# Top-k attention with a routed MLP on one core: where a batch's first block is transposed, and when reciprocals of row sums are taken

## Chip, core and metric

One core of a Trainium2 chip runs the whole kernel. The metric is device time in microseconds (us), the median of several runs. TensorE is PE in the profile (PEld its weight loads), VectorE is DVE, ScalarE is ACT, GpSimd is POOL and SyncE is SP. A "q" behind a name (SPq) is the engine's queue of DMA issues and waits.

## What is computed

Two stages in float32. First attention over 8 batches, 8 heads, 576 rows, head size 64, where each row keeps only its 32 largest scores. Then each of the 4608 rows (512 wide) goes to one of 8 experts, a two-layer MLP of width 1024, and is scaled by the gate's weight.

```python
def _attn_ref(q, k, v):
    scores = scale * np.matmul(q, k.transpose(0, 1, 3, 2))
    kth = np.partition(scores, -top_k, axis=-1)[..., -top_k:-top_k + 1]
    scores = np.where(scores >= kth, scores, -1000000000.0)
    attn = np.exp(scores - np.max(scores, axis=-1, keepdims=True))
    attn = attn / (np.sum(attn, axis=-1, keepdims=True) + 1e-09)
    return np.matmul(attn, v)

def _moe_ref(x, w_gate, w1, w2):
    logits = x @ w_gate
    expert_idx = np.argmax(logits, axis=1)
    ...
    for e in range(E):
        h = np.maximum(x_sorted[lo:hi] @ w1[e], 0.0)
        y_sorted[lo:hi] = h @ w2[e]
    ...
    return gate_w[:, None] * y
```

## The kernel before, in words

**The two stages are interleaved.** The attention's work is cut into 144 slots, 18 for each batch: a slot is two tiles of 128 query rows, as a rule the same rows of the two heads of a "unit" (4 units a batch; one slot in nine takes the remaining 64 rows of both heads of two units). As soon as a batch's rows are finished they are sorted by expert into a table in DRAM (x_rows), and full blocks of 128 rows of one expert are run through the MLP in between the slots of the next batches. What is left over when the attention is done runs behind it.

**A slot** i of the main loop `loop()` (lines 916 to 972) goes through these steps, and each engine gets its instructions in that order:
- DVE: `fold` (L290, L292: maximum h and minimum l of two halves of the scores s), then `search`: 8 MAX8 (L338) with MATCH_REPLACE8 (L345) between them find the 32nd largest score of each row; `fold_on` (L298, L300) prepares the next slot before the last round. Between these, `tick()` puts in one small instruction of other work at a time, from the list `aside`.
- ACT: `low` (L354) from DVE's threshold, two relu passes (L370); POOL: two subtractions (L379) that mark what is not kept.
- ACT: copies of the scores of slot i + 3 from PSUM (L283).
- PE: `turning(i - 1)`, the transposition of the previous slot's weights (wTm L398, with ACT's copies wT L404 or L402; then wTl, L411 or L409, with the copy wTt L419 or L417).
- PE: a few `pieces` of the current MLP block, in two helpings before and one behind the next steps.
- ACT: `weights`, the exponentials (L387) with row sums z.
- PE: `multiply(i + 4)`, scores of a later slot (sc L276).
- In some slots a step of `ending` (from line 803) of a finished unit: products with v (po L432, copy oT L434), the transposition back and the gate's logits (px L443, copy xl L450), `divisors` (ACT rz L454 and L455, DVE reciprocal L457), and on POOL `logits` and `rows` (L465 to L478) that multiply by the reciprocals.

PE, ACT and DVE run in the order in which the loop writes their instructions; SP's order of DMA issues follows from the same order. There are three slots of scores in advance (AHEAD = 3), so DVE may run ahead of PE and ACT until it needs an s (L290) that ACT has not copied; and ACT may run ahead of DVE until it needs a threshold (L354).

**An MLP block** (`block`, L673) has 16 pieces. Its rows xg must first be transposed by PE (`turned`: xtp L662) and copied to SBUF by ACT (xTs L664). Then come 8 pieces of the first layer (ph L687, copy hT L692), and 8 of the second (py L702, scaled copy y L716, scattered to the output by POOL, L708). Copies that ACT owes to a block wait in a list `due` and are written down by `evacuate()`. In the middle of a block `following()` transposes the rows of the next one, if its load is old enough (`landed`, 3 slots). For the first block of a batch there is no block before it that could do so; then `block` itself calls `turned`, yields "pause", and its next step starts with `evacuate("xT")`. This happens in slot 13 of a batch, in the helpings ahead of `weights`.

**Loads** on SP: for each block xg (L642) and two weight tiles w (L634, L636), issued by `ahead()` when the block before the last one loaded begins; for each unit qkb (L141) and vb (L245).

**Divisors.** In `ending`, `next(div)` writes ACT's two rz instructions, and `aside.append(div)` at once puts the DVE reciprocal on the list, so that it goes into the next search. `through(div)` at the place "rows" makes sure that it has been written before POOL's `logits`.

Of the kernel before, what the change touches and what calls it, by code (L numbers as in the profile page):

```python
# [35 lines left out]
def kernel(  # L36
# [265 lines left out]
    aside = []  # L302
# [365 lines left out]
    def evacuate(upto=None):  # L668

        while due and (upto is None or upto in [kind for kind, _ in due]):  # L670
            due.pop(0)[1]()
# [62 lines left out]
    with fast:  # L734
# [10 lines left out]
        current = None  # L745
        left = clock = 0

        def landed(n):
            return clock is None or clock - n.at >= ON_CHIP
# [16 lines left out]

        def following():
            put_stores()
            if loaded and landed(loaded[0]):
                turned(loaded[0])  # L770

        def pieces(n):
            nonlocal current, left
            while n > 0 and left > 0:
                if current is None:
                    if not landed(loaded[0]):
                        break
                    current = block(loaded.pop(0), following, stores.append)
                    ahead()
                if clock is None:  # L780
                    evacuate()
                step = next(current)
                if step == "pause":
                    if clock is not None:
                        break
                    continue
                if step == "last":
                    current = None
                n -= 1
                left -= 1  # L790
            return n
# [11 lines left out]
        def ending(b, u):  # L803

            nonlocal left
            n = unit[b * U + u]
            if u == 0:
                x_of[b] = k.xp.tile([P, KC, XW], F32, name="x")
                in_turn(token_ids(x_of[b][:, :, Dm + 1].bitcast(I32), b))
                lg_of[b] = k.small.tile([P, KC, E], F32, name="lg")  # L810
            x, lg = x_of[b], lg_of[b]
            out_steps = outputs(n, x)
            yield "products"
            next(out_steps)
            yield "relu"
            next(out_steps)
            if u % 2 == 0:
                yield "relu"
            div = divisors(n)
            next(div)  # L820
            aside.append(div)
            yield "products"
            next(out_steps)
            if b * U + u + 2 < len(units):
                load_values(unit[b * U + u + 2])
            yield "relu"
            next(out_steps)
            yield "products"
            next(out_steps)
            yield "relu"  # L830
            next(out_steps, None)
            yield "rows"
            through(div)
            logits(n, lg)
            rows(n, x)
            if u < U - 1:
                return
            yield "small"
            r = choice(lg)
            aside.append(r.steps)  # L840
            yield "weights"
            yield "turn"
            through(r.steps)
            nc.scalar.activation(lg, lg, AF.Exp)
            yield "products"
            ranks(r)
            yield "small"
            steps = places(r, x)
            aside.append(steps)
            yield "relu"  # L850
            nc.scalar.copy(run, r.run)
            yield "pool"
            through(steps)
            scatters.extend(scattering(r, x))
            if b == B - 1:
                scatter(KC)
                slot_i = k.small.tile([1, 2, NSLOT], I32, name="slot_i")
                through(table(slot_i, SURE, False))
                firsts = [(slot_i[0:1, 0, j:j + 1], slot_i[0:1, 1, j:j + 1]) for j in range(SURE)]
                ready = load_rows(SimpleNamespace(), firsts[0][1], True)  # L860
            new = LAST - SURE if b == B - 1 else new_of[b]
            if new:
                slot_i = slot_last if b == B - 1 else k.small.tile([1, 2, NSLOT], I32, name="slot_i")
                steps = table(slot_i, new, b == B - 1)
                aside.append(steps)
                yield "weights"
                yield "pool"
                yield "weights"
                yield "pool"
                through(steps)  # L870
                coming.extend((slot_i[0:1, 0, j:j + 1], slot_i[0:1, 1, j:j + 1]) for j in range(new))
            if b == B - 1:
                spare.extend(coming[ALWAYS - SURE:])
                del coming[ALWAYS - SURE:]
                assert len(loaded) == 2 and not waiting
                fill_up()
                coming[0:0] = [(firsts[0][0], ready)] + [(expert, (piece,)) for expert, piece in firsts[1:]]
                scatter(0)
# [27 lines left out]
        def loop():  # L906
            nonlocal credit, rate, clock
            for i in range(min(AHEAD, len(work))):
                multiply(i)
                s_of[i], steps = scores(got_of.pop(i))  # L910
                for step in steps:
                    step()
            multiply(AHEAD)
            f_of[0] = fold(s_of[0])
            fold_on(f_of[0])
            for i, (b, g) in enumerate(work):
                tiles = tiles_of(i)
                u, tile = g[0]
                if tile == 0 and u % 2 == 0:
                    open_unit(tiles[0][0])  # L920
                if tails(tiles):
                    open_unit(tiles[1][0])

                then = lambda: None
                if i + 1 < len(work):
                    f_of[i + 1] = fold(s_of[i + 1])
                    then = lambda: fold_on(f_of[i + 1])
                low, nbias, doubts = search(tiles, s_of[i], f_of.pop(i), then)
                at_place("small")
                w_of[i] = depths(s_of[i], low)  # L930
                less(s_of.pop(i), w_of[i])
                doubts()
                put_stores()
                scatter(1)
                at_place("pool")
                at_place("relu")
                at_place("rows")
                at = i % per_batch
                if at == FIRST and b:
                    rate = new_of[b - 1] * PIECES / (U * NT)  # L940
                credit += rate * len(g)
                room = left
                if b == B - 1 and at >= ARRIVED:
                    room -= KEEP
                    credit = room / (len(work) - i)
                share = {0: 0.5, 1: 1.2, 2: 1.6, 3: 0.5, 2 * NC: 1.4}[tile]
                now = max(0, min(int(credit * share + 0.5), room))
                credit -= now
                clock = i
                if i + AHEAD < len(work):  # L950
                    s_of[i + AHEAD], steps = scores(got_of.pop(i + AHEAD))
                    for step in steps:
                        step()
                evacuate()
                at_place("turn")
                turns = turning(i - 1) if i else iter(())
                next(turns, None)
                part = min(BETWEEN, now - now // 2)
                rest = pieces(part)
                next(turns, None)  # L960
                rest = pieces(now - now // 2 - part + rest)
                weights(tiles, w_of[i], nbias)
                next(turns, None)
                evacuate()
                if i + AHEAD + 1 < len(work):
                    multiply(i + AHEAD + 1)
                if tile == NC - 1:
                    end = ending(b, u)
                    late.append([end, next(end)])
                at_place("products")  # L970
                at_place("weights")
                credit = min(credit + pieces(now // 2 + rest), 6 * rate)

            for _ in turning(len(work) - 1):
                pass
            assert len(late) == 1
            clock = None
            for place in late[0][0]:
                if place == "rows":
                    pieces(4)  # L980
            kept = left - ALWAYS * PIECES
            assert kept >= 0, kept
            k.apart = True
            pieces(kept)
# [135 lines left out]
```

## Time and profile before

| what | value |
|---|---|
| runs before, us | 1373.47, 1373.48, 1373.33, 1374.39 (median 1373.48) |
| the profiled execution | 1374.84 us, span of its instructions 1373.2 us |
| busy PE / DVE / ACT / POOL | 1232.6 / 1084.2 / 931.8 / 661.3 us |
| granted PE clock, mean | 0.953 |
| the last search ends | 1090.8 us; what follows is MLP blocks |
| HBM traffic | 208.72 MB read, 22.33 MB written |

Busy shares in 40 slices are tenths (9 is 90% or more), each slice 34.3 us. A line of the timeline has the start, the duration, engine, line, operation, output<-input, shapes and count, and in brackets the idle time of the engine before it and what ended it. PE's counts are twice those of the program, since each float32 matmul is two instructions in the trace. The chain of waits that ended last covers only the last 28 us (it begins at 1344.85) and lies within the last MLP blocks.

### The profile page before, as it was taken

To read this page: it belongs to the slowest core of one execution; us is meant where nothing else is said; L and a number is where in the kernel's file an instruction comes from. 1 tells how busy PE (TensorE), PEld (TensorE's weight loads), DVE (VectorE), ACT (ScalarE), POOL (GpSimd) and SP (SyncE) were. 2 spreads that over 40 slices of the span, in tenths; PEclk is the share of its full clock that TensorE was granted. 3 is DMA by queue.
4 is the path that set the end of the run, shared out by engine and by line. 5 is a ranking of instruction groups with operands and counts; after the bars stand their busy time and mean duration, and the time that the engine had idled before them with its cause. 6 is when DMAs were issued, how large, how long until landed. Compare 5 with 4: busy or idle time off the path is not lost. (4 is left out here: it accounts for less than half of the span.)

```text
span 1373.2 us, 24487 instructions
## 1 busy us (share of the span) xinstructions
PE 1232.6 (90%) x7666; PEld 839.0 (61%) x7666; DVE 1084.2 (79%) x4591; ACT 931.8 (68%) x2113; POOL 661.3 (48%) x805
## 2 busy tenths in 40 slices
PE   5777677677799999999999999999999999999995
PEld 3444444444467666767676666667676676776773
DVE  7999999999999999999999999999999720000000
ACT  4788877877888888887877788887777821111110
POOL 3455547555654666566556655665556621000000
PEclk9788887888999999999999999999999999999998
DMA  2000011001573277427554573367443759999880
GB/s 82 29 29 29 28 36 55 29 29 44 185 290 135 76 252 253 151 64 265 214 193 148 183 276 131 110 214 283 166 167 110 272 182 357 388 323 329 304 319 19
DMA packets 102221, 231.68 MB, mean 169 GB/s; under 512 B 5183, under 2 KB 25919, under 8 KB 102081
## 3 DMA queue, kind: packets, MB, share of 16 engines
q1 hardware_dynamic: 95328, 209.76, 43.6%
q0 software_dynamic: 6464, 19.97, 4.0%
q8 instruction: 62, 1.02, 0.3%
q14 instruction: 79, 0.64, 0.1%
q10 hardware_dynamic: 288, 0.30, 0.1%
HBM read 208.72 MB, written 22.33 MB: 168 GB/s over the span
## 5 line engine op out<-in xcount | busy, mean ns | idle before, releaser
L379 POOL TENSOR_TENSOR w<-s,w 128x576 f32<-128x576 f32 x288 | 409.6, 1443 | 432.0 <-ACT w L370 432.0
L687 PE MATMUL ph<-xTs,w 128*128 128x128 f32 x2560 | 308.6, 276 | 7.2 <-ACT xTs L664 6.0
L687 PEld LDWEIGHTS ph<-xTs,w 128*128 128x128 f32 x2560 | 297.4, 192 | 27.7 <-issue 18.4
L702 PE MATMUL py<-w,hT 128*128 128x512 f32 x640 | 292.2, 596 | 0.0
L338 DVE MAX8 tops<-scr 128x8 f32<-128x168 f32 x864 | 245.8, 316 | 0.0
L276 PE MATMUL sc<-qkb 64*128 64x288 f32 (+1 forms) x1280 | 220.1, 469 | 9.7 <-ACT s L283 5.2
L387 ACT ACTIVATE w<-w,nbias 128x576 f32<-128x576 f32 x288 | 223.9, 791 | 3.5 <-POOL w L379 2.5
L370 ACT ACTIVATE w<-s,low 128x576 f32<-128x576 f32 x288 | 207.6, 768 | 4.7
L398 PE MATMUL wTm<-turn,w 128*128 128x128 f32 x1152 | 173.2, 291 | 34.7 <-ACT xl L450 21.6
L398 PEld LDWEIGHTS wTm<-turn,w 128*128 128x128 f32 x1152 | 135.1, 148 | 95.2 <-issue 35.5
L999 DVE CAST any_i<-pd 1x1 int32<-1x1 f32 x1 | 0.1, 147 | 237.4 <-PE pd L997 237.4
L702 PEld LDWEIGHTS py<-w,hT 128*128 128x128 f32 x640 | 114.4, 190 | 117.6 <-issue 116.5
L345 DVE MATCH_REPLACE8 scr<-tops,scr 128x168 f32<-128x168 f32 x576 | 177.2, 312 | 0.0
L283 ACT COPY s<-sc 128x576 f32<-128x576 f32 x288 | 169.0, 640 | 10.6 <-PE sc L276 10.6
L404 ACT COPY wT<-wTm 128x512 f32<-128x512 f32 x256 | 139.3, 603 | 39.4 <-PE wTm L398 39.0
L276 PEld LDWEIGHTS sc<-qkb 64*128 64x128 f32 (+1 forms) x1280 | 117.9, 195 | 72.8 <-issue 25.5
L432 PE MATMUL po<-wT,vb 128*64 128x288 f32 x1024 | 157.1, 455 | 0.4 <-ACT wTt L419 0.4
L708 POOL DMA_INDIRECT out_dram<-y,xg x40 | 43.1, 1078 | 212.9 <-ACT y L716 199.6
L329 DVE MAX8 few<-l 128x8 f32<-128x288 f32 x288 | 127.4, 442 | 0.0
L692 ACT ACTIVATE hT<-ph 128x512 f32<-128x512 f32 x80 | 48.6, 608 | 108.7 <-PE ph L687 108.7
L290 DVE TENSOR_TENSOR h<-s 128x576 f32<-128x576 f32 x144 | 117.1, 813 | 5.9 <-ACT s L283 5.9
L432 PEld LDWEIGHTS po<-wT,vb 128*64 128x64 f32 x1024 | 74.9, 151 | 76.2 <-issue 28.1
(116 smaller groups left out, 1430.7 us busy)
## 6 DMA issues: line engine op xcount, KB each, us to landing
w<-in_moe_w_dram SPq DMA_DIRECT2D x80, 2048.0 KB, 9.6
qkb<-in_qk_dram SPq DMA_DIRECT2D x31, 608.0 KB, 4.4
xg<-x_rows SPq DMA_DIRECT2D x40, 257.0 KB, 10.0
vb<-in_v_dram SPq DMA_DIRECT2D x32, 320.0 KB, 3.2
x_rows<-blank SPq DMA_DIRECT2D x5, 257.0 KB, 15.8
x_rows<-blank POOLq DMA_DIRECT2D x4, 257.0 KB, 9.1
x_rows<-x,posi POOLq DMA_INDIRECT x40, 3.2
out_dram<-y,xg POOLq DMA_INDIRECT x40, 6.1
```

Of the source, the lines that this page charges most:

```text
L276: nc.tensor.matmul(ps[rows, j, 0:HF], n.q[d, cols], n.k[d, keys], start=True, stop=True)
L283: lambda m=m, ps=ps: nc.scalar.copy(s[:, m, :, :], ps[:, :, 0:HF]) for m, ps in enumerate(got)
L338: nc.vector.max(out=tops[:, m, r * 8:(r + 1) * 8], in_=src[m])
L345: nc.vector.match_replace(out=scr[:, m, :], in_to_replace=tops[:, m, r * 8:(r + 1) * 8], in_values=src[m], imm_value=NEG,)
L370: nc.scalar.activation(w[:, m, :], s[:, m, :, :].rearrange("p j k -> p (j k)"), AF.Relu, scale=-STEEP, bias=low[:, m:m + 1],)
L379: k.last_pool = in_turn(nc.gpsimd.tensor_tensor(w[:, m, :], s[:, m, :, :].rearrange("p j k -> p (j k)"), w[:, m, :], op=ALU.subtract)).ins
L387: nc.scalar.activation(w[:, m, :], w[:, m, :], AF.Exp, scale=scale, bias=nbias[:, m:m + 1], accum_out=n.z[:, c:c + 1])
L398: nc.tensor.transpose(pm[:, c * P:(c + 1) * P], w[:, m, first:first + P], ident)
L404: nc.scalar.copy(wT[:, :, m, q], pm4)
L432: nc.tensor.matmul(po[r, 0:HF], n.v[:, c, r], rhs, start=(c == 0), stop=(c == KC - 1))
L687: nc.tensor.matmul(ph[:, f, :], n.w1[:, 0, dt, fc * P:(fc + 1) * P], n.xT[:, dt, :], start=(dt == 0), stop=(dt == DT - 1),)
L702: nc.tensor.matmul(py, hT[:, f, :], n.w2[:, 0, f, :], start=(f == 0), stop=(f == FT - 1))
```

## The change

Three places. `following()` no longer transposes rows that are transposed already, and the loop calls it in each slot in which no block is running. `pieces` begins a block inside the loop only if its rows have been transposed (after the loop `block` does it, as before). And the reciprocal of `divisors` is put on the list two steps later in `ending`.

```diff
--- before.py
+++ after.py
@@ -766,14 +766,14 @@
 
         def following():
             put_stores()
-            if loaded and landed(loaded[0]):
+            if loaded and landed(loaded[0]) and not hasattr(loaded[0], "xT"):
                 turned(loaded[0])
 
         def pieces(n):
             nonlocal current, left
             while n > 0 and left > 0:
                 if current is None:
-                    if not landed(loaded[0]):
+                    if clock is not None and not hasattr(loaded[0], "xT"):
                         break
                     current = block(loaded.pop(0), following, stores.append)
                     ahead()
@@ -818,13 +818,13 @@
                 yield "relu"
             div = divisors(n)
             next(div)
-            aside.append(div)
             yield "products"
             next(out_steps)
             if b * U + u + 2 < len(units):
                 load_values(unit[b * U + u + 2])
             yield "relu"
             next(out_steps)
+            aside.append(div)
             yield "products"
             next(out_steps)
             yield "relu"
@@ -961,6 +961,8 @@
                 rest = pieces(now - now // 2 - part + rest)
                 weights(tiles, w_of[i], nbias)
                 next(turns, None)
+                if current is None:
+                    following()
                 evacuate()
                 if i + AHEAD + 1 < len(work):
                     multiply(i + AHEAD + 1)
```

From line 964 on the line numbers are two higher in the changed kernel.

## Prediction

> **What bounds the kernel now.** I read the page's busy slices first. VectorE is full up to the 27th slice and idle behind it; TensorE is full from about the 12th slice to the end.
>
> ```profile
> PE   5777677677799999999999999999999999999995
> DVE  7999999999999999999999999999999720000000
> ```
>
> Both are above 90% for two thirds of the span, so I cut the span into stages. The columns are the length, then busy us (and instructions) of PE, PEld, DVE, ACT, POOL, then granted clock, DMA share and GB/s.
>
> ```profile
> 380.00:660.00 280.00, 273.01 (x1836) 189.16 (x1835) 278.77 (x1199) 236.18 (x540) 165.26 (x200) 1.00 0.53 190
> 660.00:893.00 233.00, 230.17 (x1511) 158.41 (x1512) 229.51 (x940) 190.04 (x437) 141.07 (x163) 1.00 0.49 172
> 893.00:1091.00 198.00, 193.40 (x1297) 135.56 (x1296) 193.38 (x800) 160.35 (x367) 121.42 (x139) 1.00 0.58 207
> 1115.00:1373.00 258.00, 241.78 (x1393) 176.03 (x1391) 5.29 (x33) 39.43 (x67) 23.67 (x26) 0.98 0.82 291
> ```
>
> From 660 to 1091 us PE and DVE are each idle for under 3%. A large gain or loss has no room there unless something new is waited for. Next, who waits for whom, in total, times, longest:
>
> ```profile
> DVE rz L457 <- ACT rz L455: 10.9, 7, 6.0
> DVE h L290 <- ACT s L283: 5.9, 6, 1.6
> PE ph L687 <- ACT xTs L664: 6.0, 6, 1.1
> ```
>
> The first and third line are what the two edits touch. Between 600 and 1090 us the rz waits are 1.58 us at 682, 0.68 at 794, 1.57 at 963 and 0.69 at 1075; the longest, 6.01, is at 1103, behind the last search; 0.37 is left for the two others. The xTs waits are one per batch: 0.65 at 375, then 1.06 at 644, 791, 925, 1072 and one near 509.
>
> Which engine leads? The timeline tells it by two kinds of wait. When DVE is behind, ACT waits at low L354 for DVE's tops; when PE and ACT are behind, DVE waits at h L290 for ACT's s.
>
> ```profile
> 700.38 1.81 DVE L290 TENSOR_TENSOR h<-s 128x576 f32<-128x576 f32 x1 [0.91 <-ACT s L283]
> 794.50 0.22 DVE L457 RECIPROCAL rz<-rz 128x10 f32<-128x10 f32 x1 [0.68 <-ACT rz L455]
> 890.12 0.20 ACT L354 ACTIVATE low<-tops 128x2 f32<-128x2 f32 x1 [1.65 <-DVE tops L338]
> 892.13 0.66 PE L398 MATMUL wTm<-turn,w 128*128 128x128 f32 x4 [1.05 <-ACT oT L434]
> ```
>
> At 700 DVE stands where ACT (and so PE) lets it. At 890 it is the other way round: ACT waits 1.65 us for DVE, and through oT PE loses 1.05 us. So 890 is a meeting point: PE time lost before it is forgiven up to 1.05 us, and DVE time gained before it counts. Behind 893 no ACT low waits for DVE for more than 0.98 us, the last at 904, and PE has no gap over 0.5 us except the two xTs waits up to 1088. From 893 to the end PE's own stream sets the time.
>
> **The change part by part.** The lists of instructions of both kernels have the same PE, ACT and POOL instructions and no POOL one moved; nothing is added.
>
> *Reciprocals.* 31 of 32 DVE reciprocals (0.20 us) go one search later; the last, after the loop, stays, and so does its 6.01 us wait. At some 7 us a slot each of the others finds its ACT operands done. In five of the batches one reciprocal falls behind the last MAX8 of its search; POOL's L465, which reads it, stands behind the POOL subtractions of that slot, which wait for that same MAX8 and then two ACT passes, so nothing is late. DVE loses its waits: 1.58 us at 682 brings nothing, since DVE then waits that much longer for s at 700. 0.68 us at 794 counts for the meeting at 890. 1.57 and 0.69 us behind 893 bring nothing as long as PE sets the end.
>
> *Transposition.* The words say "one slot ahead". The PE order says something else: at six places (one per batch) the old order xtp, wTl, ph, sc, ph becomes wTl, xtp, sc, ph. The number of ph in the slot is the same. What changes is the cover. On ACT the old order wT, wT, y, xTs, exp, exp, wTt becomes wT, wT, exp, exp, wTt, y, xTs: the copy that PE waits for goes behind two exponentials. The place at 925 us before:
>
> ```profile
> 923.96 0.27 PE L411 MATMUL wTl<-turn,w 128*128 128x128 f32 x1
> 924.03 0.73 ACT L716 ACTIVATE y<-py,xg 128x512 f32<-128x512 f32 x1
> 924.61 0.63 ACT L664 COPY xTs<-xtp 128x512 f32<-128x512 f32 x1
> 925.07 0.84 ACT L387 ACTIVATE w<-w,nbias 128x576 f32<-128x576 f32 x1
> 925.29 2.94 PE L687 MATMUL ph<-xTs,w 128*128 128x128 f32 x24 [1.06 <-ACT xTs L664]
> 926.60 0.31 ACT L419 COPY wTt<-wTl 128x128 f32<-128x128 f32 x1
> 926.75 0.27 ACT L354 ACTIVATE low<-tops 128x2 f32<-128x2 f32 x1
> 928.16 1.24 PE L276 MATMUL sc<-qkb 64*128 64x288 f32 x8
> 929.34 3.84 PE L687 MATMUL ph<-xTs,w 128*128 128x128 f32 x32
> ```
>
> Starts taken from these rows: both exponentials with their reads 925.07 to 926.60 = 1.53 us; wTt 0.15; y 0.58; xTs until ph starts 0.68. After the change ACT is free at 924.03 for the exponentials (their w was ready at 923.48), and ph can start at 924.03 + 1.53 + 0.15 + 0.58 + 0.68 = 926.97. PE is through with wTl and xtp at 925.29 - 1.06 = 924.23, as before, and has sc (929.34 - 928.16 = 1.18) up to 925.41. So PE waits 926.97 - 925.41 = 1.56 us instead of 1.06. Cross-check by the end of the slot: the next wTm starts at 933.01 now and would at 926.97 + 2.87 + 3.67 = 933.51. **+0.50 us a place.** The same sum at 791 gives 792.63 + 1.98 + 2.78 = 797.39 against 796.89, again +0.50. sc comes 2.8 us earlier, which only ends a 0.63 us ACT wait for it; ACT then waits for wTm (2.52 us) anyway. The place at 375 lies where ACT waits for DVE each slot, the one near 509 ahead of such waits (1.65 us at 609): nothing is left of them.
>
> *SyncE queue.* At most of these places the load of xg moves behind the next qkb load, which waits for sc. Neither is in a hurry: the xg issued at 924.33 lands at 938.99 and is transposed at 971.8; the qkb of 929.47 is read five slots on. Behind both stands the w1 load, which PE's ph releases at 934.97; xg's long issue (4.26 us) set behind 929.82 ends at 934.1. I take 0; without this cover w1 would come late by xg's 4.26 us, and it lands at 945.6 for a block that begins after 971.8.
>
> *Sum.* DVE at 890: +0.50 (the place at 644, handed on at 700) - 0.68 = -0.18. PE at 892: two places (644, 791), 1.00 - 1.05 = -0.05. The later one counts: -0.05. Then the places at 925 and 1072: +1.00. **+0.95 us.** The profiled run took 1374.84 us (span 1373.2), so 1375.8 beside it; it lies 1.36 above the median of 1373.48, so I predict **1374.4 us** as a median. No row shows the new order, so I bound a place from both sides. ACT takes its instructions in order and both exponentials now stand ahead of xTs, which leaves no gain to be had; if they and y ran fast enough for the old wait, the place would cost 0. At the other end an exponential also waits for POOL's w: the longest such wait in the whole trace is 0.5 us, so +1.00. I take +0.50, since all its terms are rows of that very place. With 0 the sum is -0.68 (DVE at 890 decides: 0 - 0.68; PE 0 - 1.05); with +1.00 it is 2.00 - 1.05 + 2.00 = +2.95.
>
> **Rivals.** (1) *The xTs wait is gone*, as the change's words suggest. Then DVE reaches 890 by 1.06 + 0.68 = 1.74 earlier, PE could by more, and 925 and 1072 give 2.12: -3.86, 1369.6 us. For it: the six waits are there. Against it: xTs stands behind both exponentials, and one sc of 1.18 us is all that PE has meanwhile. This is also the case in which the change would do what it says. 4%.
>
> (2) *DVE is the bound after all* and its waits count in full: 1.58 + 0.68 + 1.57 + 0.69 + 0.37 = 4.9, 1368.6 us. For it: DVE is full from 40 to 640 us. Against it: the h waits right behind the rz waits, and ACT at low is 0.4 to 5.9 us behind DVE in all slots from 911 us on. 4%.
>
> (3) *DVE, further ahead, runs into POOL* and is late at 890. Two-input DVE instructions are stretched when a POOL subtraction lies beside them:
>
> ```profile
> 778.50 2.98 POOL L379 TENSOR_TENSOR w<-s,w 128x576 f32<-128x576 f32 x2 [1.50 <-ACT w L370]
> 780.15 1.65 DVE L300 TENSOR_TENSOR hl<-h 128x288 f32<-128x288 f32 x1
> ```
>
> L300 takes 0.48 us on average, 1.65 here: 1.2 us lost. From 794 on DVE is ahead of POOL by 0.68 + 0.50 us more, so that in the slots up to 860 the subtraction shifts towards L298 and L300. Against it: each such loss takes the lead away again, so it can hardly repeat in every slot. It decides from two such slots (2.4 - 0.18 + 1.00 = +3.2); three give +4.4: 1376.7 to 1377.9 us. 12%. The Trainium skill ("SBUF — State Buffer", section "Who interferes with whom") says that a VectorE instruction with two SBUF inputs and a GpSimd one that reads SBUF exclude each other, and the second waits for the whole of the first; the stretched L300 agrees. By that rule taken alone every slot in which they newly meet would pay, and the sum would be rival 3's.
>
> **How the numbers follow.** Forecast 80%, rivals 4, 4 and 12%. About 0.2% (2.7 us) is what a measurement of this kernel can tell from no change; the forecast lies well inside, rivals 1 and 2 are faster, 3 slower. So faster 8%, same 80%, slower 12%. The range goes from the lower end of a place's cost less the spread of the four runs (1374.39 - 1373.33 = 1.06), -0.68 - 1.06 = -1.7, to the three slots of rival 3, +4.4, which takes in the +2.95: 1371.7 to 1377.9 us.
>
> **What would show it.** Right: the waits of ph for xTs are some 1.5 us each at four places, xTs stands behind wTt on ACT, sc ahead of ph; the rz waits are gone but the 6 us one; DVE's h waits grow near 700 and 980. PE's gap at 892 shrinks to near 0. Wrong: no xTs waits left (rival 1), no h waits (2), more L298 and L300 over 1 us between 794 and 890 and a longer ACT wait for tops at 890 (3), or a new PE wait for a weight load.

## The result and the profile after

The changed kernel takes 1375.77 us (median of 40 runs, 1373.71 to 1378.83) against 1373.83 us (60 runs, 1371.55 to 1376.14). The ratio is 1.0015, with a 95% interval from 1.0011 to 1.0019: 1.5 to 2.6 us longer, 1.94 by the medians. The forecast was +0.95 us, about half of that. The direction came as forecast, and so did a loss within 0.2%, but the experiments show that the two halves of the sum were wrong in opposite directions.

Of the page's busy slices, those of TensorE and VectorE again:

```profile
PE   5777677677699999999999999999999999999995
DVE  8999999999999999999999999999999820000000
```

They hardly differ from before. The windows for the two stages in which both engines are full (length, then busy us and instructions of PE, PEld, DVE, ACT, POOL, then clock, DMA share, GB/s):

```profile
660.00:893.00 233.00, 229.89 (x1508) 157.76 (x1506) 231.24 (x933) 189.60 (x434) 139.51 (x162) 1.00 0.49 173
893.00:1091.00 198.00, 192.29 (x1294) 134.92 (x1295) 195.37 (x799) 159.61 (x367) 120.98 (x137) 1.00 0.58 203
```

Here is the first clue. DVE's work is the same, yet it is busy 1.73 and 1.99 us longer in these two stages (229.51 and 193.38 before), and 6.0 us longer over the span (1090.2 against 1084.2). DVE's waits fell by less than that:

```profile
DVE h L290 <- ACT s L283: 7.2, 6, 1.6
DVE rz L457 <- ACT rz L455: 6.0, 1, 6.0
```

The reciprocals' waits are gone but for the one behind the loop (10.9 to 6.0 us), as the change intends; the waits for s grew from 5.9 to 7.2. PE's wait for the transposed rows grew from 6.0 to 7.1:

```profile
PE ph L687 <- ACT xTs L664: 7.1, 6, 1.3
```

**Where the time came from.** Traces of this kernel repeat to some 0.01 us wherever nothing differs, so the two can be compared slot by slot. For each slot I took ACT's low (L354) and subtracted its time before from its time after:

| place (us, before) | shift ahead of it | shift behind it | cost |
|---|---|---|---|
| 375 | -0.07 | +0.26 | 0.33 |
| 510 | +0.33 | +0.64 | 0.31 |
| 644 | +0.72 | +1.02 | 0.30 |
| 791 | +1.03 | +1.33 | 0.30 |
| 925 | +1.41 | +1.71 | 0.30 |
| 1072 | +1.72 | +2.03 | 0.31 |

It is a staircase. Each of the six places costs 0.3 us, nothing is forgiven between them, and three further steps of 0.07 us stand at about 467, 601 and 882 us, one slot behind places where a reciprocal now follows the last MAX8 of a search (why these cost 0.07 us, and the three others of the kind nothing, I did not follow). 6 x 0.31 + 3 x 0.07 = 2.07; the last search ends 2.03 later, from -0.07: 2.10.

The span tells the opposite: 1372.4 us after (the execution took 1373.96), 1373.2 before. That is one execution against one. What differs is a stretch behind the last search in which the profiled execution of before had PE at half clock. Before, then after:

```profile
1103.00:1106.50 3.50, 3.50 (x18) 0.52 0.00 0
```

```profile
1103.00:1106.50 3.50, 2.47 (x20) 1.00 0.00 0
```

The po group of 16 that falls there took 3.78 us at half clock and 2.16 at full clock, and its short successor 0.78 and 0.66: 1.74 us. A further 1.0 us is a wait of ph for its weight load near 1156, 1.2 us before and 0.2 after. 2.03 - 1.74 - 1.0 = -0.7, near the -0.8 of the spans. I put neither down to the change: a half-clock stretch lies over the same po group in one later profile of the changed kernel too (the last run below: from 1106.2 us, the group takes 3.71 us; mean clock 0.83 from 1100 to 1110 us, as before), and the two kernels below that add only a fill on POOL have no such wait for a weight load.

### The profile page after: what moved, and what is told of

The parts are those of the page before. It is cut to its first block, busy times and chain, and to the rows that moved or that the text cites. A ratio compares the mean times of both kernels' runs of the same rounds, so it can differ in the third digit from the quotient of the medians.

```text
span 1372.4 us, 24492 instructions
## 1 busy us (share of the span) xinstructions
PE 1230.0 (90%) x7666; PEld 836.8 (61%) x7666; DVE 1090.2 (79%) x4591; ACT 931.7 (68%) x2113; POOL 663.6 (48%) x805
## 3 DMA queue, kind: packets, MB, share of 16 engines
q8 instruction: 62, 1.02, 0.3%
## 5 line engine op out<-in xcount | busy, mean ns | idle before, releaser
L379 POOL TENSOR_TENSOR w<-s,w 128x576 f32<-128x576 f32 x288 | 409.5, 1443 | 432.4 <-ACT w L370 432.4
L432 PE MATMUL po<-wT,vb 128*64 128x288 f32 x1024 | 154.3, 449 | 0.4 <-ACT wTt L419 0.4
L290 DVE TENSOR_TENSOR h<-s 128x576 f32<-128x576 f32 x144 | 115.4, 802 | 7.2 <-ACT s L283 7.2
## 6 DMA issues: line engine op xcount, KB each, us to landing
xg<-x_rows SPq DMA_DIRECT2D x40, 257.0 KB, 10.2
```

Source lines behind the costliest of these rows:

```text
L379: k.last_pool = in_turn(nc.gpsimd.tensor_tensor(w[:, m, :], s[:, m, :, :].rearrange("p j k -> p (j k)"), w[:, m, :], op=ALU.subtract)).ins
L432: nc.tensor.matmul(po[r, 0:HF], n.v[:, c, r], rhs, start=(c == 0), stop=(c == KC - 1))
```

## The experiments

Two theories. **Passed on**: what a place costs PE and ACT reaches the end in full, and what DVE gains is lost within some slots. **Forgiven**, which is the prediction's own: near 890 us (and ahead of it near 600) PE's losses are forgiven up to 1.05 us and DVE's gains count. Shifts are those of the last search; I count them from 467 us on, because half-clock stretches at 330 to 375 us differ between executions.

**One edit at a time.** The kernel before with the reciprocals alone:

```diff
             next(div)
-            aside.append(div)
             yield "products"
...
             next(out_steps)
+            aside.append(div)
             yield "products"
```

> The kernel before with the reciprocals one search later and nothing else. Three theories, all read by the moment of the last search's end (1090.8 us in the trace before, 1092.9 in the changed one) since the blocks behind it vary by themselves. PASSED ON: DVE's time, gained at the waits for rz, is lost again within some slots, at h waits and in two-input instructions that stand behind a POOL subtraction, so the last search ends within 0.15 us of before and the time is the same (ratio 0.9995 to 1.0005). FORGIVEN (the prediction's meeting point): 0.68 us are gained at the meeting at 890, so the last search ends 0.3 to 0.7 us earlier. DVE BOUND: all four waits count, 3 to 5 us earlier.

Measured: 1372.28 us (11 runs) against 1373.55; ratio 0.9995 (0.9986 to 1.0004). The shift grows by 0.18 us from 467 us on (+0.90 to +1.08), a little over the 0.15 expected of "passed on", and nothing is gained. Behind each missing wait DVE is early (by 1.5 us at 685 and at 966), and 25 us later it is not. These gains never reach the meeting at 890.

The kernel before with the transposition alone, that is the first two and the last place of the change:

```diff
+                if current is None:
+                    following()
                 evacuate()
```

> The changed kernel with the reciprocals where they were. PASSED ON: the six places cost 0.3 us each whatever lies between, and the reciprocals give nothing: last search 2.0 us later than before (1.8 to 2.2), ratio 1.001 to 1.002. FORGIVEN: only the two places behind the meeting at 890 and what DVE is late there count: about 0.6 to 1.3 us later. If the reciprocals were what costs the time, 0.

Measured: 1374.08 us (11 runs); ratio 1.0011 (1.0002 to 1.0020). The shift goes from -0.24 to +1.34, +1.58 for the five places behind 467 us (with the first, -0.57 to +1.34, 1.91). The steps are the staircase above, without the three of 0.07. The two edits add up: 0.18 + 1.58 = 1.76, and the changed kernel has 1.70 from 467 us on. So the loss is the transposition's.

**What in the place costs.** The prediction blamed the copy xTs, which stands behind both exponentials on ACT. This kernel is the changed one with the transposition and the copy ahead of the exponentials; sc still goes ahead of ph on PE:

```diff
-                weights(tiles, w_of[i], nbias)
-                next(turns, None)
                 if current is None:
                     following()
+                    evacuate()
+                weights(tiles, w_of[i], nbias)
+                next(turns, None)
                 evacuate()
```

> The changed kernel, but the transposition and its copy are written ahead of the exponentials: PE has the changed kernel's order (wTl, xtp, sc, ph), ACT the old one (y, xTs, then the exponentials). COPY BEHIND THE EXPONENTIALS IS THE PRICE (all theories of mine): the wait of ph for xTs, 1.29 us each, is gone or under 0.2 us, and each of the last two places gives 1.0 us against before; what the first four give depends on how far DVE can follow: last search 2 to 5 us earlier than before, ratio 0.996 to 0.999. RIVAL, the order sc before ph is the price: the waits stay near 1 us and the time stays at 1.0015.

Measured: 1366.84 us (5 runs), 0.9958 (0.9945 to 0.9972). The shift from 467 us on is -3.96. Its timeline at the place of 925 us:

```profile
920.48 0.60 PE L662 MATMUL xtp<-turn,xg 128*128 128x128 f32 x4
920.59 0.74 ACT L716 ACTIVATE y<-py,xg 128x512 f32<-128x512 f32 x1
921.01 1.24 PE L276 MATMUL sc<-qkb 64*128 64x288 f32 x8
...
921.17 0.64 ACT L664 COPY xTs<-xtp 128x512 f32<-128x512 f32 x1
921.64 0.83 ACT L387 ACTIVATE w<-w,nbias 128x576 f32<-128x576 f32 x1
922.18 5.07 PE L687 MATMUL ph<-xTs,w 128*128 128x128 f32 x43
```

The copy lies under sc, and ph follows sc with no gap: in this kernel's list of waits PE has none for xTs. PE's order in the changed kernel is good; what it lacks is the place of the copy (with the y ahead of it) on ACT. The gains are passed on as the losses were: -1.05 us a place at 510, 644, 791 and 925, of which 0.2 is given back twice (at 725 and 1006) and the rest is kept. The place at 1072 adds 0.3 us at the last search.

**Is a loss forgiven?** The kernel before, with the four transpositions of one block done four times over, in slot 67 alone (same values, 12 more PE transpositions near 509 us):

```diff
-        for dt in range(DT):
+        for dt in [d for _ in range(k.times) for d in range(DT)]:
...
+                k.times = 4 if i == 67 else 1
```

> The kernel before, where in one single slot (the first block of the fourth batch, near 509 us) the four transpositions of rows are made four times over the same values: about 1.4 us more of TensorE, once, ahead of two meetings (near 600 and 890) where ACT waits for DVE. PASSED ON: the last search ends later by nearly the whole of it, 1.1 to 1.4 us. FORGIVEN: ACT's and PE's waits for DVE take it up, 0 to 0.35 us at the last search.

Measured: 1374.12 us (10 runs), 1.0008 (0.9998 to 1.0017). The size is a miss, +0.83 us (from +1.18, which half-clock stretches at 331 and 365 us had left in this execution, to +2.01), since 0.49 us of PE's extra 1.31 (xtp takes 1.91 instead of 0.60) replace its wait for xTs, which falls from 1.06 to 0.57. But these 0.83 us are still there to the last search (+2.08), over both meetings. Forgiven is wrong.

**How a loss reaches DVE without a wait.** DVE's extra busy time had to be somewhere. Take slot 70, the first behind the place at 510, with POOL's subtractions and DVE's L298 beside them. Before, then after:

```profile
520.81 2.79 POOL L379 TENSOR_TENSOR w<-s,w 128x576 f32<-128x576 f32 x2 [3.81 <-ACT w L370]
...
522.78 1.13 DVE L298 TENSOR_TENSOR few<-h 128x288 f32<-128x288 f32 x1
```

```profile
521.45 2.79 POOL L379 TENSOR_TENSOR w<-s,w 128x576 f32<-128x576 f32 x2 [2.73 <-ACT w L370]
...
523.09 1.46 DVE L298 TENSOR_TENSOR few<-h 128x288 f32<-128x288 f32 x1
```

Without POOL beside it this L298 takes 0.44 us. It ends 0.31 us behind POOL both times: 523.91 against 523.60, and 524.55 against 524.24. POOL waits for ACT, so it is late by the 0.64 us that ACT has lost so far, and L298 starts only 0.31 later but ends 0.64 later. The list of waits shows nothing; the instruction is simply longer. To see that POOL sets this end, I delayed POOL alone, by a small fill of zeros (over zeros) between the two subtractions of slot 69, whose second one runs beside L298 above:

```diff
         for m in range(2):
+            if m and extra:
+                in_turn(nc.gpsimd.memset(blank[:, 0:256], 0.0))
...
+                less(s_of.pop(i), w_of[i], i == 69)
```

> The kernel before with one POOL instruction more, in one slot: a memset of 128x256 zeros over zeros (about 0.31 us by the memset rows of 128x128 and 128x513) between the two subtractions L379 of the slot where, in the trace before, DVE's L298 is stretched at 522.78. No semaphore ties DVE to these. DVE TIED TO POOL: L298 still ends 0.31 us behind the end of the second subtraction, so it is stretched by 0.3 us more and the end of that search comes 0.3 us later beside its neighbours; and since the next stretched instructions also end with POOL's (which is not late there), DVE is back in step within three slots and the last search ends as before, but for shifts that are there already ahead of 510 us. RIVAL (the stretch is something else, and POOL only happens to lie beside it): L298 stays at 1.13 us and nothing moves.

Measured: 1373.06 us (one execution; the trace decides here, not the time). This kernel's L381 is L379 of the others:

```profile
520.52 1.41 POOL L381 TENSOR_TENSOR w<-s,w 128x576 f32<-128x576 f32 x1 [3.80 <-ACT w L370]
...
521.87 0.31 POOL L380 MEMSET blank<- 128x256 f32 x1
...
522.14 1.41 POOL L381 TENSOR_TENSOR w<-s,w 128x576 f32<-128x576 f32 x1
...
522.49 1.38 DVE L298 TENSOR_TENSOR few<-h 128x288 f32<-128x288 f32 x1
```

POOL ends at 523.55, L298 at 523.87, again 0.32 behind it. Against this execution's shift of -0.28 that is 0.24 us late for DVE, from POOL alone. Two slots on DVE has made it up (-0.28): its next stretched instructions end with a POOL that is not late, and so they are shorter by as much. The control has the same fill in slot 81, where DVE has only MAX8, MATCH_REPLACE8 and a reciprocal beside POOL's second subtraction:

```diff
+                less(s_of.pop(i), w_of[i], i == 81)
```

> The same memset in a slot where the subtractions lie beside one-input DVE instructions only (near 610 us in the trace before). DVE TIED TO POOL BY TWO-INPUT INSTRUCTIONS: nothing of DVE moves in that slot (under 0.05 us). RIVAL (any POOL work delays DVE or the exponentials): the end of that search or of the next comes about 0.3 us later.

Measured: 1373.33 us (one execution); no shift (-0.22 before, -0.21 and -0.22 after). It is the overlap, not POOL's extra work, that DVE feels.

Nor is L298 at 522.78 a special case. L298 takes 0.44 us as a rule. All 25 that take over 0.52 us in the kernel before end 0.31 or 0.32 us behind an instruction of POOL, and so do all 32 in the changed kernel. The kernel with the transposition alone shows DVE's whole way, since no reciprocal moves in it. From 510 us to the last search the shift at the end of DVE's instructions (here DVE's own, not that of ACT's low) changes in these places only, but for a few hundredths:

| at (us, before) | shift ahead | behind | what became longer |
|---|---|---|---|
| 522.78 | -0.26 | +0.07 | L298, 1.13 to 1.46 us |
| 666.24 | +0.08 | +0.38 | L298, 0.44 to 0.74 us |
| 803.52 to 811.48 | +0.40 | +0.69 | L298, L290 and L298, 2.66 to 2.96 us in sum |
| 947.22 | +0.71 | +1.00 | L298, 0.44 to 0.73 us |
| 1084.50 | +1.02 | +1.34 | L298, 0.53 to 0.85 us |

So DVE takes over each loss of PE and ACT within 25 us, and by 890 all that was lost ahead of it.

**Are the reciprocals worth anything in the better order?** The kernel with the copy ahead, with the reciprocals as before:

```diff
             next(div)
+            aside.append(div)
             yield "products"
...
             next(out_steps)
-            aside.append(div)
             yield "products"
```

> The kernel with the copy ahead of the exponentials, with the reciprocals where they were before. If the reciprocals never matter (DVE's waits for rz only stand in for stretched instructions and h waits): ratio as with them moved, 0.995 to 0.997, last search from 470 us on gaining the 4.0 to 4.4 us that the other kernel gained, within 0.3. If, now that PE is earlier, DVE's waits for rz bind: up to 2 us of the gain are lost, ratio 0.997 to 0.998.

Measured: 1368.89 us (10 runs) against 1372.62; 0.9976 (0.9967 to 0.9986), shift from 467 us on -3.90. Since this ran beside another run of the kernel before, the three were run once more side by side: the copy ahead,

> The kernel with the copy ahead of the exponentials and the reciprocals moved, again, beside the one with the old reciprocals and the changed kernel on one chip. Their traces end the last search 3.96 and 3.90 us earlier than before (counted from 470 us on), so if the reciprocals give nothing the two have the same time, ratio 0.996 to 0.998 both; if moving them gives what the first two measurements differ by, this one is 2 us or more faster than the other.

the same with the reciprocals as before,

> The copy ahead of the exponentials, old reciprocals, again: the same as its neighbour within 0.1% if the reciprocals give nothing.

and the changed kernel.

> The changed kernel itself beside them: ratio 1.001 to 1.002, 2 us slower than before and 5 to 7 us slower than the two with the copy ahead.

Measured, against 1373.77 us: 1367.97 (5 runs; 0.9965, 0.9951 to 0.9979), 1368.57 (6 runs; 0.9967, 0.9955 to 0.9979) and 1375.59 (11 runs; 1.0015, 1.0006 to 1.0024). The reciprocals make no difference that shows (intervals overlap almost entirely; shifts of -3.96 and -3.90), and the version that beats both kernels is the copy ahead, by about 5 us. Of these, 3.9 stand at the last search; the rest lies in the blocks behind it, and I did not follow it there.

## Why the prediction was half right

**The mechanism at a place was right.** The changed kernel at 925 us (all shifted by the +1.41 of the earlier places):

```profile
925.31 0.60 PE L662 MATMUL xtp<-turn,xg 128*128 128x128 f32 x4
925.43 0.82 ACT L387 ACTIVATE w<-w,nbias 128x576 f32<-128x576 f32 x1
925.84 1.24 PE L276 MATMUL sc<-qkb 64*128 64x288 f32 x8
926.96 0.29 ACT L419 COPY wTt<-wTl 128x128 f32<-128x128 f32 x1
927.11 0.73 ACT L716 ACTIVATE y<-py,xg 128x512 f32<-128x512 f32 x1
...
927.69 0.63 ACT L664 COPY xTs<-xtp 128x512 f32<-128x512 f32 x1
...
928.37 6.52 PE L687 MATMUL ph<-xTs,w 128*128 128x128 f32 x56 [1.29 <-ACT xTs L664]
...
934.72 1.04 PE L398 MATMUL wTm<-turn,w 128*128 128x128 f32 x8
```

xTs stands behind both exponentials, wTt and y. ph was to start at 926.97, with the shift 928.38; it starts at 928.37. **The mis-sized term** is what follows: I added 2.87 and 3.67 = 6.54 us for ph in two pieces, each with a change to or from sc; in one piece it takes 934.72 - 928.37 = 6.35 (that the changes cost the 0.19 us was not tried by itself). So the place costs 1.67 (ph's later start, 928.37 - 1.41 - 925.29) - 1.18 (sc, no longer between) - 0.19 = 0.30 us, not 0.50. That the wait reads 1.29 and not 1.56 costs nothing: sc starts 0.20 us later than I reckoned, and ph starts when the copy lets it.

**The step that failed is the meeting**, "890 is a meeting point: PE time lost before it is forgiven up to 1.05 us, and DVE time gained before it counts", and with it "nothing is left of them" for the places at 375 and 509. After the change:

```profile
891.52 0.20 ACT L354 ACTIVATE low<-tops 128x2 f32<-128x2 f32 x1 [1.65 <-DVE tops L338]
...
893.54 0.66 PE L398 MATMUL wTm<-turn,w 128*128 128x128 f32 x4 [1.11 <-ACT oT L434]
```

PE's gap was to shrink to near 0. It is 1.11 us, 1.05 before, and ACT waits 1.65 us as before: PE, ACT and DVE arrive there 1.41 us later together. I had taken DVE for an engine on its own between two h waits. It is not: POOL follows ACT, and L298, L300 and L290, where POOL holds them up, end only behind it; so a late ACT makes DVE late in the next slot where they meet, as in slot 70 and in the table above. The place at 644 reached DVE in this way at 666, and not at 700 through the wait for s. The other way round, a DVE that is early runs into POOL. At 683 its 1.49 us are gained; at 698, where L298 took 0.45 us before,

```profile
696.22 2.77 POOL L379 TENSOR_TENSOR w<-s,w 128x576 f32<-128x576 f32 x2 [4.94 <-ACT w L370]
...
697.79 1.52 DVE L298 TENSOR_TENSOR few<-h 128x288 f32<-128x288 f32 x1
...
701.41 1.81 DVE L290 TENSOR_TENSOR h<-s 128x576 f32<-128x576 f32 x1 [1.25 <-ACT s L283]
```

it takes 1.52 us, 1.07 of the gain, and the wait for s behind it is 0.34 longer than before (1.25 against 0.91). So "DVE then waits that much longer for s at 700" had the right end and mostly the wrong place. "0.68 us at 794 counts" was wrong in the same way: in the reciprocals-only kernel DVE stands at +0.71 behind it, and at +0.99 one slot later, where it had been before. Over the whole trace, L298 takes 76.3 us before and 81.7 after, 5.4 more. L300 has 1.2 more (69.1 to 70.3) and L290 1.7 less (117.1 to 115.4): 4.9 us in sum, against 4.9 us of rz waits gone.

Rival 3 named this stretch, with 12%, but as an extra price of two or three slots. It is a coupling: it adds nothing to the path by itself (the reciprocals alone cost 0.18 us), and it keeps a slack from being used. The Trainium skill ("SBUF — State Buffer", section "Who interferes with whom") has the exclusion of such a VectorE instruction and a GpSimd one that reads SBUF; L298, with 0.44 us of its own, ends 0.31 us behind POOL in three kernels, which agrees with it to 0.13 us. By the rule as I used it, each new overlap would pay; the runs show that it pays only as far as DVE was early.

**The sum, mended**: places 0.31 instead of 0.50, six instead of two that count, nothing for the meeting, and 3 x 0.07 for the reciprocals that I costed at 0: 2.07 us. (Those behind the last MAX8 of a search are six in the trace, not five.) With the right 0.31 and my meeting the forecast would have been DVE 0.31 - 0.68, PE 0.62 - 1.05, so -0.37 + 0.62 = +0.25: the oversized term hid part of the failed step. That the forecast came within 1 us of the change is to that extent luck.

**Right as written**: the SyncE queue costs nothing (the w1 load's issue moves from 934.97 to 936.68, 1.71 later like all else in that slot); the rz waits are gone but the 6 us one; the h waits grow near 700 and 980; neither rival 1 nor 2 came. Rival 1's reason against, "xTs stands behind both exponentials", is what the copy-ahead kernel took away, and it then gave the gain that rival 1 hoped for.

**Left open**: whether the 1.05 us at 890 would be forgiven without the tie. A kernel whose POOL subtractions never lie beside DVE's two-input instructions was not tried.

## What to carry to other kernels

A wait that has gone is not yet time: follow the engine's lead slot by slot, and look at instructions that became longer, since an engine that is blocked inside an instruction counts as busy. Before you count on slack at a meeting point, make sure that the two engines run freely up to there, and look for a third engine that ties them. When a producer is moved earlier, move the copy behind it as well, past what stands in that engine's order: here that is the difference between +2 and about -5 us.

## What the runs showed of the hardware

DVE's two-input instructions end as if they had started about 0.13 us ahead of POOL's end: L298 and L300 (0.44 us) 0.31 behind it, L290 (0.73 us) 0.61 behind the end of POOL's L478 (602.73 against 602.12 in the kernel before). Where L298 starts within 0.2 us of POOL's start it is the other way round: at 731.78 in the kernel before L298 takes 0.43 us, and the two subtractions from 731.58 take 3.66 us instead of the 2.79 of those at 520.81.

Stretches in which TensorE's clock is granted at half speed are 3.4 us long, or a multiple (6.8, 10.2, 13.65), and two executions of one program can differ in them: of the two profiles of the changed kernel one has such a stretch at 1106.2, the other none between 362 us and the last blocks. The Trainium skill ("TensorE: Matmul & The Clock Gate", section "What's actually happening") speaks of a free-running activity window of some 3.4 us; the lengths agree. The traces also show what stands ahead of such a stretch: PE was busy for 1.69 of the 3.40 us up to 1103.0 in the kernel before, and for 1.69 of the 3.40 up to 1106.2 in the later profile of the changed kernel. In its other profile, cut into pieces of 3.41 us in step with its own stretches, PE is busy for over 2 us of each piece from 420 us to the last blocks. No run tried this by itself. In this kernel one stretch is worth 1.7 us and by that alone can turn round a comparison of two single spans.
